# Half products of a DFT as two matmuls of 256 columns instead of one of 512

## The chip, the cores and the metric

One NeuronCore of a Trainium2 chip runs the whole kernel. The metric is the time on the device in microseconds of one execution; lower is better. The core's engines are TensorE (matmuls; the profile calls its matmuls PE and its weight loads PEld), VectorE (DVE), ScalarE (ACT), GpSimd (POOL) and SyncE (SP), which issues the DMAs.

## What is computed

Two branches over one sequence `x` of 2048 rows and 512 columns, mixed by a gate; everything is float32.

```
a = x @ dft_hid_re.T ;  b = x @ dft_hid_im.T
y = dft_seq_re @ a - dft_seq_im @ b                 # real part of a 2-D DFT
q, k, v = heads(x @ wqkv)                           # 32 heads of 16
o = softmax(q k^T / 4) v ;  att = merge(o) @ wo
g = sigmoid((x * gate_w).sum(-1))
out = g * y + (1 - g) * att
```

The change touches the line of `y`, the sequence transform: two products of a 2048 x 2048 matrix with a 2048 x 512 matrix.

## The kernel before

**Precision.** Matmuls of the transforms run in a rounded float32 type. Each factor is split into a high part and the rest, and a product is made of three: high times high, high times rest, rest times high. So one stationary block `h1` (the high part of 128 x 128 of the DFT matrix) is used with the two moving tiles `t[:, 0]` and `t[:, 1]` (high part and rest of 128 rows of `a` or `b`, 512 columns), and `l1` (its rest) with `t[:, 0]`.

**Half products.** TensorE's array has 128 rows. A product over 128 rows is made as two over 64 rows each, in different segments (below), both added into the same PSUM bank. While one half of the array's rows does a half product, the other half does a matmul of the attention, which needs at most 64 rows.

**Stages.** The first 207 us make q, k, v and the imaginary part `b` of the transform over the columns. Then a long middle stage works through the attention's units, two heads at a time, and lays the rest of the transforms beside them. Its work is written out by hand as patterns of slots:

```
FULL = "a5 s4 a2 s0 a3 s6 a5 s4 s1 s0 s2 a6 a3 a4 s5 a1 | |"
```

A pattern is one segment. `a` is a score tile for the row maxima (`a_tile`, matmul at L294, reduced by VectorE at L296), `s` is a score tile for the exponentials (`scores`, matmul at L805, exponentiated by ScalarE at L806), the digit is the PSUM bank, and `|` is the matmuls with the values (`pv`, L851). In each of the 16 slots of FULL one score goes to one half of the rows, and one half product of the sequence transform to the other. The scores come first in the program's order in the first 15 slots and last in the sixteenth. Segments come in pairs: in the second the halves of the rows change places, and the same 16 products get their other half. `take(seq, 16)` gives a pair its 16 products, `segment` sends them out with the scores, and `Chain.mm` (L476) makes the matmul. The first product of a segment waits for a user of the scores of the segment before, so that the two halves of a product don't follow too closely; `segment` puts that dependency on the instruction that `issue` returns.

`dft` yields the products of the sequence transform in their order: for the real part of the DFT matrix (`c = 0`, the first half) and then the imaginary one (`c = 1`, the second half), for each of 16 output tiles `tt`, for each of 16 row tiles `s`, the three products. An output tile is one chain of 48 products in the bank `psD`, 3 pairs of segments long. `dft_next` follows the third product of each `s`: at the end of a chain ScalarE copies the bank out (L531 for `c = 0`, L534 for `c = 1`), and every fourth time GpSimd splits the next chunk of the DFT matrix (L460, L461) and SyncE loads a further one (L450). There are 48 pairs of FULL segments for each half of the transform.

Before the FULL segments come 13 pairs of another pattern with the products of `real` (real part of the transform over the columns), and after them the output projections; both use `Chain.mm` too, with moving tiles 512 columns wide.

The matmuls of the values are float32 as they are, with 17 weights in each of four column groups of the array, and use all 128 rows.

Of the kernel before, what the change touches and what calls it, by code (L numbers as in the profile page):

```python
# [17 lines left out]
D = 512  # L18
# [13 lines left out]
def mix_kernel(ctx: ExitStack, tc: tile.TileContext, xa_t, xa, wqkv, w_hid, w_seq, wo, gate_w, out):  # L32
# [5 lines left out]
    nc = tc.nc  # L38
# [156 lines left out]
    with tc.tile_pool(name="qk", bufs=1, reuse_waits="tile") as pool:  # L195
# [38 lines left out]
        for tb in range(4):  # L234
# [4 lines left out]
            for c in range(2):  # L239
                if tb == 0 and c == 0:  # L240
                    pss = [bank() for _ in range(4)]
                    for kt in range(KT):
                        x = xab[tb][:, :, :, kt * P:(kt + 1) * P]
                        for i, (w, v) in enumerate(((wh, 0), (wl, 0), (wh, 1))):
                            for ct in range(4):
                                nc.tensor.matmul(pss[ct], w[:, c, kt, ct * P:(ct + 1) * P], x[:, :, v],
                                                 start=kt == 0 and i == 0, stop=kt == KT - 1 and i == 2)
# [198 lines left out]
    def c_load(i):  # L446
        if i < len(chunks):
            c, tt, ch = chunks[i]
            raws[i] = work.tile([P, 4, P], F32, name="craw", tag="yr") if i < 2 else spare(i % 2, F32, "craw")
            nc.sync.dma_start(raws[i], w_seq[c, tt, ch])  # L450
# [14 lines left out]
    class Chain:  # L465
# [6 lines left out]
        def mm(self, st, mv, half, stop):  # L472
            if not self.begun:
                self.ps = self.pool.tile([P, 512], F32, name=self.name)
            r = slice(None) if half is None else slice(64 * half, 64 * half + 64)
            i = nc.tensor.matmul(self.ps, st[r], mv[r], start=not self.begun, stop=stop)  # L476
            self.begun = True
            return i

    def real():  # L480

# [8 lines left out]
    def real_next(s, t, chain):  # L490
# [9 lines left out]
        if s == NT - 1:  # L500
# [2 lines left out]
            c_split(2)  # L503
            c_load(4)

    def dft():

        for c in range(2):
            for tt in range(NT):
                chain = Chain(psD, "d", 48)  # L510
                yr = []
                for ch in range(4):
                    i = (c * NT + tt) * 4 + ch
                    h1, l1 = hls.pop(i)
                    if c == 1 and ch == 0:
                        yr.append(work.tile([P, D], F32, name="yr"))
                        nc.sync.dma_start(yr[0], yr_d[tt])
                    for k in range(4):
                        s = 4 * ch + k
                        t = ab[s]  # L520
                        yield chain, h1[:, k], t[:, 0], None
                        yield chain, h1[:, k], t[:, 1], None
                        yield chain, l1[:, k], t[:, 0], partial(dft_next, c, tt, s, t, chain, yr)

    def dft_next(c, tt, s, t, chain, yr):
        if c == 0 and tt == NT - 1:
# [150 lines left out]
    def proj(hf, cts, pools, qts=range(8)):  # L677

        for qt in qts:
            t = hf * 8 + qt  # L680
            chain = Chain(*pools[qt % len(pools)], 3 * len(cts))
            for ct in cts:
                h1, l1 = oh[hf, ct][qt]
                for i, (st, mv) in enumerate(((h1, 0), (h1, 1), (l1, 0))):
                    last = ct == cts[-1] and i == 2
                    yield chain, st, wos[0][:, mv, ct], partial(proj_next, hf, cts, t, chain) if last else None
# [205 lines left out]
    for hf in range(2):  # L892
        for ct in range(4):
            n = 3 if hf and ct == 3 else 4
# [125 lines left out]
    first = proj(0, (0, 1, 2), one * 5 + side[::-1], range(7))  # L1020
    run_plan(0)
    gate()
    hid, seq = real(), dft()


# [59 lines left out]
    for u in range(valued + 2, UNITS, 2):  # L1085
        run_plan(u)
        clock = nc.vector if u == 498 else nc.gpsimd
        i = 0
# [57 lines left out]
```

## Time and profile before

| | |
|---|---|
| two timed runs | 1655.51 and 1655.59 us, median 1655.55 us |
| profiled execution, first to last instruction | 1653.7 us |
| TensorE matmuls, busy | 1646.4 us (100%), 13082 |
| TensorE weight loads, busy | 995.5 us (60%), 13082 |
| VectorE, busy | 1372.1 us (83%) |
| ScalarE, busy | 1264.0 us (76%) |
| GpSimd, busy | 683.8 us (41%) |
| granted clock of TensorE | 0.999 |
| FULL segments of the first half of the transform | 348.92 to 899.90 us, 550.98 us |
| FULL segments of the second half | 899.90 to 1451.30 us, 551.40 us |

The profile is one execution, and its times are counted from its first instruction. A row of a group gives the line of the kernel, the engine, the operation, the tiles written and read, the shape (partitions x elements), the count, and then the busy time in us and the mean length of one in ns. A row of the timeline gives start and length in us first. Lengths of matmuls are modelled and overlap, so what a matmul takes in a row of them is read from one start to the next.

### The profile page before, as it was taken

What the parts mean: (1) busy time and instruction counts of PE and PEld (TensorE: products, weight loads), DVE (VectorE), ACT (ScalarE), POOL (GpSimd) and SP (SyncE); (2) the same over time, 40 slices, a digit from 0 to 9 for tenths busy, and PEclk for the clock granted to TensorE, in tenths of its full rate; (3) what the DMA queues carried; (4) which work ended last, traced back from release to release, by engine and by line L of the source; (5) the groups of instructions that cost most, each with busy time, mean ns of one, the idle gap of its engine ahead of it and who ended that gap; (6) DMA issues with size and microseconds to landing.
All of it is one profiled execution on the core that took longest, in us unless ns stands there. A gap on an engine that the chain in (4) does not pass through costs nothing.

```text
span 1653.7 us, 34501 instructions
## 1 busy us (share of the span) xinstructions
PE 1646.4 (100%) x13082; PEld 995.5 (60%) x13082; DVE 1372.1 (83%) x2338; ACT 1264.0 (76%) x2477; POOL 683.8 (41%) x651
## 2 busy tenths in 40 slices
PE   9999999999999999999999999999999999999998
PEld 7888966655555555555555555555555555544454
DVE  5439888888888888888888888888888888899954
ACT  5312289988888788887888878888788887889996
POOL 0204634443433456434343455544444455333330
PEclk9999999999999999999999999999999999999999
DMA  9977401314141534223147535224141536371014
GB/s 287 355 164 154 160 2 28 51 39 80 58 79 47 98 94 100 71 60 71 41 97 251 106 102 119 66 67 78 51 87 59 113 104 128 130 206 27 23 46 142
DMA packets 85247, 167.17 MB, mean 101 GB/s; under 512 B 22460, under 2 KB 22716, under 8 KB 81068
## 3 DMA queue, kind: packets, MB, share of 16 engines
q1 hardware_dynamic: 84648, 164.30, 39.0%
q8 instruction: 103, 1.69, 0.5%
q10 hardware_dynamic: 432, 0.66, 0.1%
q14 instruction: 64, 0.52, 0.1%
HBM read 109.67 MB, written 55.17 MB: 100 GB/s over the span
## 4 chain that ended last, share of the span: by engine, by line
PE 99%; DMA 0%; DVE 0%; DVEq 0%; ACT 0%; SPq 0%; issue 0%
PE acc L851 28%; PE a L294 23%; PE s L805 21%; PE d L476 9%; PE s L388 3%; PE acc L805 3%; PE acc L294 2%; PE s L422 1%; PE d L388 1%; PE acc L813 1%; PE a L111 1%; PE a L109 1%; PE s L111 1%; PE s L109 1%; PE a L110 1%; PE s L110 1%
## 5 line engine op out<-in xcount | busy, mean ns | idle before, releaser
L296 DVE TENSOR_REDUCE mx<-a 128x1 f32<-128x512 f32 x1828 | 1140.8, 683 | 164.0 <-PE a L294 103.1
L806 ACT ACTIVATE pt<-s 128x512 f32<-128x512 f32 x1792 | 946.4, 628 | 15.2 <-PE s L805 11.2
L294 PE MATMUL a<-ks,qs 64*128 64x512 f32 (+1 forms) x1828 | 677.3, 410 | 0.0
L476 PE MATMUL d<-xab,ch 64*128 64x512 f32 x2016 | 648.5, 396 | 0.0
L805 PE MATMUL s<-qs,ks 64*128 64x512 f32 (+1 forms) x1792 | 583.3, 397 | 0.0
L833 POOL TENSOR_TENSOR oe<-oe,part 128x512 f32<-128x512 f32 x215 | 278.1, 1293 | 653.9 <-ACT part L832 609.3
L851 PE MATMUL acc<-pt,vt 128*17 128x512 f32 x3968 | 479.0, 595 | 0.0
L294 PEld LDWEIGHTS a<-ks,qs 64*128 64x128 f32 (+1 forms) x1828 | 324.1, 184 | 244.6 <-issue 134.4
L476 PE MATMUL d<-xab,cl 64*128 64x512 f32 x1008 | 399.7, 397 | 0.0
L805 PEld LDWEIGHTS s<-qs,ks 64*128 64x128 f32 (+1 forms) x1792 | 321.9, 184 | 84.9 <-ACT pt L806 29.6
L476 PEld LDWEIGHTS d<-xab,ch 64*128 64x128 f32 x2016 | 366.5, 184 | 9.4
L832 ACT COPY part<-acc 128x512 f32<-128x512 f32 x215 | 126.2, 587 | 196.0 <-issue 174.1
L851 PEld LDWEIGHTS acc<-pt,vt 128*17 128x17 f32 x3968 | 89.0, 96 | 228.3 <-issue 148.4
L476 PEld LDWEIGHTS d<-xab,cl 64*128 64x128 f32 x1008 | 185.6, 184 | 5.0
L461 POOL TENSOR_TENSOR cl<-craw,ch 128x512 fp32r<-128x512 f32 x126 | 162.2, 1287 | 10.1
L296 DVE TENSOR_REDUCE mx<-acc 128x1 f32<-128x512 f32 x220 | 151.8, 690 | 12.2
L806 ACT ACTIVATE pt<-acc 128x512 f32<-128x512 f32 x244 | 148.7, 609 | 0.0
L805 PE MATMUL acc<-qs,ks 64*128 64x512 f32 (+1 forms) x244 | 95.5, 391 | 0.0
L294 PE MATMUL acc<-ks,qs 64*128 64x512 f32 (+1 forms) x220 | 85.8, 390 | 0.0
L460 POOL CAST ch<-craw 128x512 fp32r<-128x512 f32 x126 | 77.0, 611 | 18.8 <-PE d L476 13.1
L476 PE MATMUL d<-wre,xab 64*128 64x512 f32 x336 | 81.7, 388 | 0.0
L476 PE MATMUL d<-wo_hl,o_hl 64*128 64x512 f32 x252 | 66.7, 395 | 0.0
(178 smaller groups left out, 1232.5 us busy)
## 6 DMA issues: line engine op xcount, KB each, us to landing
craw<-w_seq SPq DMA_DIRECT2D x128, 256.0 KB
qk<-hl SPq DMA_DIRECT2D x32, 512.0 KB
qs<-qk SPq DMA_DIRECT2D x96, 128.0 KB
ks<-qk SPq DMA_DIRECT2D x96, 128.0 KB
b<-hl SPq DMA_DIRECT2D x16, 512.0 KB
xab<-b SPq DMA_DIRECT2D x16, 512.0 KB
o<-oe SPq DMA_DIRECT2D x62, 128.0 KB
oh<-nh SPq DMA_DIRECT2D x12, 512.0 KB
```

What stands on the lines that cost most here:

```text
L109: nc.tensor.matmul(ps, sh, mh, start=first, stop=False)
L294: nc.tensor.matmul(ps, qs[p % 2][r, qt * P:(qt + 1) * P], ks[p % 2][r, kb * 512:(kb + 1) * 512], start=True, stop=True)
L296: user = nc.vector.tensor_reduce(mx[p % 2][:, h, qt, kb:kb + 1], ps, AX.X, ALU.max)
L388: i = nc.tensor.matmul(ps, st[r], mv[r], start=not half and not j, stop=half == 1 and j == 11)
L460: nc.gpsimd.tensor_copy(h1, raw)
L461: nc.gpsimd.tensor_tensor(l1, raw, h1.bitcast(F32), ALU.subtract)
L476: i = nc.tensor.matmul(self.ps, st[r], mv[r], start=not self.begun, stop=stop)
L805: nc.tensor.matmul(ps, ks[p % 2][rr, kt * P:(kt + 1) * P], qs[p % 2][rr, q0:q0 + 512], start=True, stop=True)
L806: return nc.scalar.activation(pts[u][:, 2 * qb + h], ps, AF.Exp, bias=0.0, scale=DH ** -0.5)
L832: nc.scalar.copy(part[0], acc)
L833: nc.gpsimd.tensor_tensor(total, total, part[0], ALU.add)
L851: i = nc.tensor.matmul(acc[32 * j:32 * j + 17], v[:, 16 * h:16 * h + 17], pt[:, j], start=begin, stop=done or close)
```

## The change

`Chain.mm` accepts a tuple of two moving parts, each with the output columns that it belongs to, and makes one matmul for each, with the same stationary block. The first of the two starts the accumulation, the second ends it, where the one matmul did; the first is the one returned, which carries the dependency. A new function `by_columns` cuts a moving tile into two of 256 columns. In `dft` the third product (`l1` with `t[:, 0]`) is always cut; the first two are cut where `c == 0`. Everything else stays as it is.

```diff
@@ class Chain
             r = slice(None) if half is None else slice(64 * half, 64 * half + 64)
-            i = nc.tensor.matmul(self.ps, st[r], mv[r], start=not self.begun, stop=stop)
+            first = None
+            if isinstance(mv, tuple):
+                for n, (cols, m) in enumerate(mv):
+                    i = nc.tensor.matmul(self.ps[:, cols], st[r], m[r], start=not (self.begun or n),
+                                         stop=stop and n == 1)
+                    first = first or i
+            else:
+                i = first = nc.tensor.matmul(self.ps, st[r], mv[r], start=not self.begun, stop=stop)
             self.begun = True
-            return i
+            return first
...
+    def by_columns(m):
+
+        return tuple((slice(i * D // 2, (i + 1) * D // 2), m[:, i * D // 2:(i + 1) * D // 2]) for i in range(2))
...
@@ def dft
-                        yield chain, h1[:, k], t[:, 0], None
-                        yield chain, h1[:, k], t[:, 1], None
-                        yield chain, l1[:, k], t[:, 0], partial(dft_next, c, tt, s, t, chain, yr)
+                        narrow = by_columns if c == 0 else lambda m: m
+                        yield chain, h1[:, k], narrow(t[:, 0]), None
+                        yield chain, h1[:, k], narrow(t[:, 1]), None
+                        yield chain, l1[:, k], by_columns(t[:, 0]), partial(dft_next, c, tt, s, t, chain, yr)
```

## The prediction

> **What bounds the kernel.** I read the page first, for the engine that the end hangs on, then the busy time of the long middle stage, then that stage matmul by matmul.
>
> ```profile
> span 1653.7 us, 34501 instructions
> PE 1646.4 (100%) x13082; PEld 995.5 (60%) x13082; DVE 1372.1 (83%) x2338; ACT 1264.0 (76%) x2477; POOL 683.8 (41%) x651
> PE 99%; DMA 0%; DVE 0%; DVEq 0%; ACT 0%; SPq 0%; issue 0%
> L476 PE MATMUL d<-xab,ch 64*128 64x512 f32 x2016 | 648.5, 396 | 0.0
> L476 PE MATMUL d<-xab,cl 64*128 64x512 f32 x1008 | 399.7, 397 | 0.0
> L476 PEld LDWEIGHTS d<-xab,ch 64*128 64x128 f32 x2016 | 366.5, 184 | 9.4
> ```
>
> The chain that ends last is TensorE for 99% of the span, so a change of matmuls counts at full weight unless the array does something else meanwhile. There are as many weight loads as matmuls (13082 each): one load goes with every matmul. The half products of the sequence transform are the two L476 matmul groups, 64 rows high and 512 columns wide, 2016 + 1008, and 48 more of the first two chunks stand under another tile name: 3072 half products, two for each of 1536 products. They fill the 96 pairs of segments of the full pattern, which last from 348.92 to 1451.30 us; the first half of the transform (c = 0) is the first 96 segments.
>
> ```profile
> 348.92:899.90 550.98, 550.98 (x4612) 318.87 (x4608) 485.89 (x830) 449.46 (x880) 242.37 (x228) 1.00 0.35 82
> 899.90:1451.30 551.40, 551.40 (x4614) 318.82 (x4610) 486.90 (x833) 449.55 (x880) 266.32 (x247) 1.00 0.40 99
> ```
>
> The columns after the length are the busy times of PE, PEld, DVE, ACT and POOL, then the granted clock. A segment takes 550.98 / 96 = 5.739 us and the clock is 1.00 throughout. DVE works 485.89 / 96 = 5.06 us of a segment, ACT 4.68, so TensorE sets the pace and the others have 0.68 us or more to spare. One segment, TensorE matmuls alone (start, length):
>
> ```profile
> 601.46 0.49 PE L294 MATMUL a<-ks,qs 64*128 64x512 f32 x1
> 601.47 0.49 PE L476 MATMUL d<-xab,ch 64*128 64x512 f32 x1
> 601.79 0.39 PE L805 MATMUL s<-qs,ks 64*128 64x512 f32 x1
> 601.80 0.39 PE L476 MATMUL d<-xab,cl 64*128 64x512 f32 x1
> 602.02 0.39 PE L294 MATMUL a<-ks,qs 64*128 64x512 f32 x1
> 602.03 0.39 PE L476 MATMUL d<-xab,ch 64*128 64x512 f32 x1
> 602.26 0.39 PE L805 MATMUL s<-qs,ks 64*128 64x512 f32 x1
> 602.27 0.39 PE L476 MATMUL d<-xab,ch 64*128 64x512 f32 x1
> ...
> 604.11 0.39 PE L476 MATMUL d<-xab,ch 64*128 64x512 f32 x1
> 604.11 0.39 PE L294 MATMUL acc<-ks,qs 64*128 64x512 f32 x1
> 604.33 0.39 PE L476 MATMUL d<-xab,ch 64*128 64x512 f32 x1
> ...
> 605.03 0.39 PE L476 MATMUL d<-xab,ch 64*128 64x512 f32 x1
> 605.04 0.39 PE L294 MATMUL a<-ks,qs 64*128 64x512 f32 x1
> 605.35 1.91 PE L851 MATMUL acc<-pt,vt 128*17 128x512 f32 x16
> 607.20 0.50 PE L294 MATMUL a<-ks,qs 64*128 64x512 f32 x1
> ```
>
> A product (L476) and a score (L294 or L805) start within 0.01 us of each other on the two halves of the rows and run side by side; I call that a slot. The recorded lengths (0.39) overlap, so only starts count. Products start at 601.80 and, as the fifteenth of the segment, at 605.03: 14 steps in 3.23 us, 0.231 us a slot. Over the stage it is the same: 5.739 less the values block (605.35 to 607.20, 1.85), the first slot (0.33) and the last with its drain (0.32) leaves 3.24 us for 14 steps, 0.2314 us. Single steps run from 0.22 (604.11 to 604.33) to 0.24 (602.03 to 602.27).
>
> **The change, part by part.** It moves no DMA, no wait and no operation of another engine. It makes 768 products × 2 halves = 1536 half products of the first half, and every third of the second half's 1536, 512, into two matmuls of 256 columns with the same weights: 2048 more matmuls and 2048 more weight loads. The score beside each stays 512 wide. The dependency of a segment's first product stays on the first of the two; its second follows on the same queue and waits for nothing new. The matmul that ends a chain is still its last, so the copies of L531 and L534 start where they did.
>
> The columns are the same in number. What can cost is the second load and the second start.
>
> *The load.* It can lie under the matmul before it, as the loads of a segment's start show:
>
> ```profile
> 601.46 0.18 PEld L476 LDWEIGHTS d<-xab,ch 64*128 64x128 f32 x1
> 601.57 0.19 PEld L476 LDWEIGHTS d<-xab,cl 64*128 64x128 f32 x1
> 601.80 0.18 PEld L476 LDWEIGHTS d<-xab,ch 64*128 64x128 f32 x1
> 1644.05 0.97 PEld L739 LDWEIGHTS s<-pairsum,oe 128*128 128x128 f32 x8 [0.25 <-ACT oe L733]
> 1644.08 1.08 PE L739 MATMUL s<-pairsum,oe 128*128 128x64 f32 x8
> ```
>
> The load for the next product (601.57) starts 0.11 us after the one before, while the product of the same half that began at 601.47 is still on the array, and the one after that starts at 601.80 together with its predecessor's matmul: a half takes its next weights behind its own running matmul. How short can a load with its matmul be? L739 has matmuls of only 64 columns, each with a load of 128 weights: eight loads begin in 0.97 − 0.19 = 0.78 us, 7 steps of 0.111 us. Two loads thus need 0.22 us: less than the slot of 0.2314. The second load stays hidden; if that cover were gone it would cost the whole 0.11 us, 2048 × 0.11 = 225 us.
>
> *The start.* No matmul of 256 columns is in this trace, so I bound it by its neighbours in width. With no second stream beside it a matmul of 512 columns with its load takes:
>
> ```profile
> 92.95 14.21 PE L422 MATMUL s<-wv,xab 128*128 128x512 f32 x62
> ```
>
> (14.21 − 0.39) / 61 = 0.2266 us. So of a slot's 231.4 ns, 4.8 ns come from the company of the other half. There are stretches without them:
>
> ```profile
> 402.08 0.39 PE L476 MATMUL d<-xab,ch 64*128 64x512 f32 x1
> 402.98 0.39 PE L476 MATMUL d<-xab,cl 64*128 64x512 f32 x1
> ```
>
> The second row is the fourth product after the first: 0.90 / 4 = 0.225 us a slot, with both halves busy. For what a further start adds, the low end is nothing. The high end is the spread of one and the same instruction, 0.225 to 0.24 us, 15 ns: that much can a step lose by the way its start falls. I take the middle, 7 ns (an estimate). Alone, a narrow pair then takes 226.6 + 7 = 233.6 ns, 2 ns more than the 231.4 at which the score beside it goes anyway; so 4.8 of the 7 lie beside the score, as long as the company of the score does not cost the narrow pair its 4.8 ns as well. 2048 × 2 ns = 4.1 us; without that cover it would be 14 us.
>
> *A narrow matmul in the middle of a wide one.* The second of the pair starts when the score is half done. That the halves can run so is shown in an earlier stage, where a product and a score start 0.12 us apart and neither loses its pace (L476 217.18 to 217.41, L805 217.06 to 217.30):
>
> ```profile
> 217.06 0.39 PE L805 MATMUL s<-qs,ks 50*128 50x512 f32 x1
> 217.18 0.39 PE L476 MATMUL d<-wre,xab 64*128 64x512 f32 x1
> 217.30 0.39 PE L805 MATMUL acc<-qs,ks 50*128 50x512 f32 x1
> 217.41 0.39 PE L476 MATMUL d<-wre,xab 64*128 64x512 f32 x1
> ```
>
> *First and last slot, values.* The first slot is long because its load lies open (601.46 to 601.57); the second narrow matmul there finds its load hidden under the first. The last slot ends with the wide score (605.04) before the values. Nothing there changes.
>
> *The sum.* Against the profiled execution, 1653.7 + 4.1 = 1657.8 us of span. The two timed runs (1655.51 and 1655.59 us, median 1655.55) stand 1.85 us above that span, so the forecast is 1659.6, rounded to **1659 us**. Its own range, 0 to 6 ns a slot, is 1655 to 1668.
>
> **The rivals.**
>
> *Faster: the halves get out of each other's way.* The 4.8 ns of company may come from two 512-column streams that run in step. If narrow products bring all narrowed slots to 226.6 ns, 2048 × 4.8 = 9.8 us are won: 1646 us. It decides where the narrow pair itself fits into 226.6 ns, that is where a further start costs nothing. For it: the score's 512 columns alone would allow it. Against: the two streams that stand half a matmul apart at 217.06 keep 0.23 to 0.24, so falling out of step is not enough. With the 225 of the good stretch it would be 1642.
>
> *Slower: every start is paid.* If the steps of 0.24 are what an ill-placed start costs, and each of the two narrow matmuls is as exposed as the one wide one was, a slot grows by 6 ns (its mean above the 225 of the good stretch) to 15: 12 to 31 us, 1668 to 1686, 1677 in the middle. It decides from the point at which the pair exceeds the 231.4 of the score. For it: the products and the scores slow down together in the rows above. Against: the single stream at L422 has no such spread, so the start as such is not the cause.
>
> *Much slower: a straight line, or the issue.* If the time of a matmul with its load lay on the line from 111 ns at 64 columns to 226.6 at 512, one of 256 would take 161 ns, a pair 322, 91 ns over the slot: 186 us, 1842 us. And if TensorE's issue set the pace (a segment has 96 loads and matmuls, 59.8 ns each), 128 of them would take 7.65 us in the first half, and the whole change would cost 4096 × 59.8 ns = 245 us: 1900 us. Against the line: the row of 64 columns is the loads' own pace. Against the issue: L422's stage needs only two instructions per 226.6 ns and a slot four in 231.4, so it isn't their number that sets the step.
>
> A fixed part in each matmul is also what the Trainium skill states, in TensorEngine Tiling (Array Packing), section Instruction Overhead, against this change: each matmul has some 60 cycles of overhead. At the 2.4 GHz that TensorE: Matmul & The Clock Gate gives, that is an estimated 25 ns a start, 51 us, 1707 us. By the same clock 512 columns are 213 ns, and L422's 226.6 leave 13 ns over them; the trace does not bear the rule out for matmuls that follow one another, and 256 columns are in any case not in it.
>
> *That the change doesn't do what it says* would be equal weights loaded once for both narrow matmuls: L422 has neighbours with equal weights too, and loads and matmuls are still 13082 each, so I give it nothing of its own; it would only make the forecast surer.
>
> **How the numbers follow.** The forecast (1655 to 1668) has 0.47, the faster rival 0.23, every start paid 0.23, the last two together 0.07, for what can bend the line part of the way as well. The range must leave out no more than 2 in 10: it takes in the faster rival from 1643 and the slower up to its end, with a little beyond, and leaves out the long shots and the edges of both, about 0.12. About 2% (33 us) is what a measurement of this kernel can tell from no change: slower than 1688.7 is 0.07 and a little of the third case, 0.08; faster than 1622.4 has no mechanism with a price, 0.01; within it 0.91.
>
> **What would show it.** In the changed profile TensorE should have 2048 more matmuls and loads (15130 each), the narrow ones as 64x256. In a segment of the first half the second narrow product should start about 0.115 us after the first, in the middle of the score, and the score's step should be 0.231 to 0.235 us; the segments of the second half should lie between that and 5.744 us. The step at 0.227 would prove the faster rival, 0.24 to 0.246 the slower. If the load of the second narrow product starts only when the first has ended, the cover has failed, and the step is 0.34. DVE's and ACT's busy time should not move. I am wrong if 256 columns cost far more than half of 512, which no row here measures, or if the score waits for the product beside it.

## The result and the profile after

| | before | after |
|---|---|---|
| two timed runs, median | 1655.55 us | 1670.22 us (1670.13 and 1670.32) |
| ratio after / before | | 1.0091, 95% interval 1.0072 to 1.0110 |
| profiled execution, first to last instruction | 1653.7 us | 1668.5 us |

The kernel became 14.7 us slower, 0.9%: clearly more than nothing, and less than the 2% bound. That is 7.2 ns for each of the 2048 further matmuls. The forecast was 1659 us; the time lies 11 us above it, inside the range given (from 1643 to a little beyond 1686), but outside the forecast's own 1655 to 1668. It is the slower rival's territory (1668 to 1686).

The page of the changed kernel: span, busy times, the chain that ended last, and the groups of half products.

```profile
span 1668.5 us, 38597 instructions
PE 1660.5 (100%) x15130; PEld 1123.8 (67%) x15130; DVE 1373.0 (82%) x2338; ACT 1264.3 (76%) x2477; POOL 683.8 (41%) x651
PE 99%; DMA 0%; DVE 0%; DVEq 0%; issue 0%
L479 PE MATMUL d<-xab,cl 64*128 64x256 f32 x2016 | 405.5, 281 | 0.0
L483 PE MATMUL d<-xab,ch 64*128 64x512 f32 x1024 | 331.6, 398 | 0.0
L479 PE MATMUL d<-xab,ch 64*128 64x256 f32 x1984 | 327.8, 283 | 0.0
```

TensorE has 15130 matmuls and 15130 loads, 2048 more of each. DVE, ACT and POOL have the instructions and busy times they had. TensorE is still 99% of the chain, so its own steps must account for the whole loss. The two halves of the transform, as windows over the changed kernel (length, then busy time of PE, PEld, DVE, ACT, POOL, then the granted clock):

```profile
349.30:912.68 563.38, 563.38 (x6148) 409.24 (x6145) 486.27 (x830) 449.45 (x880) 242.81 (x228) 1.00 0.34 81
912.68:1466.15 553.47, 553.47 (x5124) 356.68 (x5120) 487.15 (x832) 449.54 (x880) 265.86 (x247) 1.00 0.40 98
```

Before, both windows together were 550.98 + 551.40 = 1102.38 us, 5.741 us a segment in each half. Now a segment takes 563.38 / 96 = 5.869 us in the first half (+0.127) and 553.47 / 96 = 5.765 in the second (+0.024). The sum is 1116.85, so 14.5 of the 14.8 us of span lie in these 192 segments, 12.2 of them in the first half. The clock is 1.00 as before. One segment of the first half, TensorE's matmuls (start, length; "x2" is the two narrow ones of a product in one row):

```profile
601.59 0.50 PE L294 MATMUL a<-ks,qs 64*128 64x512 f32 x1
601.59 0.50 PE L479 MATMUL d<-xab,ch 64*128 64x256 f32 x2
601.92 0.39 PE L817 MATMUL s<-qs,ks 64*128 64x512 f32 x1
601.93 0.40 PE L479 MATMUL d<-xab,ch 64*128 64x256 f32 x2
602.15 0.39 PE L294 MATMUL a<-ks,qs 64*128 64x512 f32 x1
602.17 0.40 PE L479 MATMUL d<-xab,cl 64*128 64x256 f32 x2
...
605.17 0.38 PE L294 MATMUL a<-ks,qs 64*128 64x512 f32 x1
605.29 0.40 PE L479 MATMUL d<-xab,ch 64*128 64x256 f32 x2
605.61 0.62 PE L863 MATMUL acc<-pt,vt 128*17 128x512 f32 x4
```

Read the two columns of starts apart. The scores go from 601.92 to 605.17 in 14 steps: 0.232 us, the pace they had. The products go from 601.93 to 605.29 in 14 steps: 0.240 us. They begin the second slot together and are 0.12 us apart in the sixteenth. Before, score and product ended side by side; now the products' half of the array ends last, and the values (605.61) wait for it. The single narrow steps are 120 ns with hardly any spread (the middle 90% of 2784 steps in the first half are all 120). So the loss is 14 × (0.240 − 0.2314) = 0.12 us a segment, on the products' side alone.

In the second half every third product is narrow:

```profile
1104.01 0.40 PE L479 MATMUL d<-xab,cl 64*128 64x256 f32 x2
1104.24 0.39 PE L483 MATMUL d<-xab,ch 64*128 64x512 f32 x1
1104.48 0.39 PE L483 MATMUL d<-xab,ch 64*128 64x512 f32 x1
1104.71 0.39 PE L479 MATMUL d<-xab,cl 64*128 64x256 f32 x2
```

Three slots take 0.70 us, 0.233 each, and the narrow one is no longer than the wide ones. So all three are longer than the 0.231 of before: over all segments of this half the narrow pair takes 232.7 ns, the wide product after it 233.5 and the one before the next pair 232.7. The loss of a segment there, 0.024 us over 16 / 3 narrow slots, is 4.5 ns for each of them, and most of it lies in the wide products; in the first half it is 0.127 / 16 = 7.9 ns.

### The profile page after: what moved, and what is told of

It reads as the page before. It is cut to its first block, busy times and chain, and to the rows that moved or that the text cites. A ratio compares the mean times of both kernels' runs of the same rounds, so it can differ in the third digit from the quotient of the medians.

```text
span 1668.5 us, 38597 instructions
## 1 busy us (share of the span) xinstructions
PE 1660.5 (100%) x15130; PEld 1123.8 (67%) x15130; DVE 1373.0 (82%) x2338; ACT 1264.3 (76%) x2477; POOL 683.8 (41%) x651
## 4 chain that ended last, share of the span: by engine, by line
PE 99%; DMA 0%; DVE 0%; DVEq 0%; issue 0%
PE acc L863 28%; PE a L294 19%; PE s L817 16%; PE d L479 15%; PE d L483 6%; PE s L388 3%; PE acc L817 2%; PE acc L294 2%; PE s L422 1%; PE d L388 1%; PE acc L825 1%; PE a L110 1%; PE a L109 1%; PE s L110 1%; PE s L109 1%; PE a L111 1%
## 5 line engine op out<-in xcount | busy, mean ns | idle before, releaser
L479 PE MATMUL d<-xab,cl 64*128 64x256 f32 x2016 | 405.5, 281 | 0.0
L479 PEld LDWEIGHTS d<-xab,cl 64*128 64x128 f32 x2016 | 338.6, 186 | 5.7
L483 PE MATMUL d<-xab,ch 64*128 64x512 f32 x1024 | 331.6, 398 | 0.0
L479 PE MATMUL d<-xab,ch 64*128 64x256 f32 x1984 | 327.8, 283 | 0.0
L479 PEld LDWEIGHTS d<-xab,ch 64*128 64x128 f32 x1984 | 272.7, 188 | 0.0
L461 POOL TENSOR_TENSOR cl<-craw,ch 128x512 fp32r<-128x512 f32 x126 | 162.2, 1287 | 10.1
L483 PEld LDWEIGHTS d<-xab,ch 64*128 64x128 f32 x1024 | 156.7, 185 | 0.0
```

The source lines that it names most:

```text
L461: nc.gpsimd.tensor_tensor(l1, raw, h1.bitcast(F32), ALU.subtract)
L479: i = nc.tensor.matmul(self.ps[:, cols], st[r], m[r], start=not (self.begun or n), stop=stop and n == 1)
L483: i = first = nc.tensor.matmul(self.ps, st[r], mv[r], start=not self.begun, stop=stop)
```

## The experiments

Ten kernels in four groups: where the loss sits, what a matmul costs by its columns, what its weights do, and which half of the array owns the price. Where a kernel has one run, it is read by its segments, which agree between kernels to about 0.01 us where nothing is changed (5.736 to 5.744 us for wide second halves). The unchanged work ahead of the full segments ends at 349 us in some kernels and at 351 in others, so one total can be 2 us off for that alone.

### One half of the transform at a time

**All products narrow in the first half, all wide in the second.**

```diff
-                        yield chain, l1[:, k], by_columns(t[:, 0]), partial(...)
+                        yield chain, l1[:, k], narrow(t[:, 0]), partial(...)
```

> The products of the first half of the sequence transform stay cut in two, those of the second half are all one matmul again (1536 further matmuls instead of 2048). In the changed kernel a segment of the first half took 5.869 us against 5.741 before, 96 of them. Start theory (every product matmul pays some 13 ns besides its columns, so two of 256 take 2 x 120 = 240 ns where the slot had 231, and the products' half sets the pace): the first half keeps its 96 x 0.127 = 12.2 us, the second gives back its 2.3 us: 1667.8 us. Equal price for each further matmul (14.67 us / 2048 = 7.2 ns): 1655.55 + 11.0 = 1666.6 us. Second-half segments back at 5.741 us by both.

Measured: 1669.42 us (four runs, 1667.71 to 1670.03), ratio 1.0082 (1.0068 to 1.0096).

```profile
351.00:914.37 563.37, 563.37 (x6148) 409.27 (x6144) 486.26 (x830) 449.45 (x880) 242.60 (x228) 1.00 0.35 80
914.37:1465.19 550.82, 550.82 (x4612) 321.06 (x4608) 487.08 (x832) 449.55 (x880) 265.82 (x247) 1.00 0.40 99
```

Its segments take 5.868 us in the first half and 5.738 in the second: the first half's loss is that of the full change, and the second half's is gone. The 1.6 us over the expected total lies ahead of the segments, which begin at 351.0 us here and at 349.3 in the changed kernel.

**Every third product narrow in both halves.**

```diff
-                        narrow = by_columns if c == 0 else lambda m: m
+                        narrow = lambda m: m
```

> Only every third product is cut, in both halves (1024 further matmuls). Start theory with a catch-up (between two cut products the two wide ones can run at the 226.6 ns of a lone stream, so the mean of three stays near the score's 231): as the changed kernel's second half, 24 ns a segment: 192 x 24 ns = 4.6 us, 1660.1 us. Equal price of 7.2 ns each: 7.3 us, 1662.9 us. A price of 7.9 ns each, as in the first half of the changed kernel: 8.1 us, 1663.7 us.

Measured: 1660.93 us (six runs), ratio 1.0034 (1.0022 to 1.0046).

```profile
348.71:902.47 553.76, 553.76 (x5126) 356.77 (x5122) 486.26 (x830) 449.58 (x880) 242.68 (x228) 1.00 0.35 82
902.47:1455.95 553.48, 553.48 (x5125) 356.32 (x5121) 487.18 (x832) 449.59 (x880) 265.95 (x247) 1.00 0.40 98
```

Both halves take 5.77 us a segment (the mean is 5.767), as the second half of the change does. An equal price of 7.2 ns for each narrow slot would make 5.780; the segments speak against it, and so does the median (1662.9 us were expected then), though the interval of the total reaches to 1663.2. Spread thin, a narrow product costs about 5 ns, and here too the wide products beside it step at 233 ns and not at 231. Why they do is open.

**Two of three narrow in the first half, all narrow in the second.**

```diff
-                        narrow = by_columns if c == 0 else lambda m: m
-                        yield chain, h1[:, k], narrow(t[:, 0]), None
+                        narrow = by_columns if c == 1 else lambda m: m
+                        yield chain, h1[:, k], by_columns(t[:, 0]), None
```

> First half: two of three products cut (first and third), second half: all of them (2560 further matmuls). Start theory with catch-up: 240, 240 and 226.6 ns make 235.5 a slot against 231.4, 66 ns a segment, 6.3 us for the first half; the second half all cut, as the first half of the changed kernel, 12.2 us: 1674.1 us, first-half segments 5.807 us, second-half segments 5.869 us. Price in proportion to the number cut (7.9 ns each): first-half segments 5.826 us, 1675.9 us. If it mattered which of the two halves of the transform is cut, second-half segments would differ from 5.869 us.

Measured: 1676.39 us (four runs), ratio 1.0126 (1.0112 to 1.0140).

```profile
349.63:908.88 559.25, 559.25 (x5636) 389.71 (x5633) 486.27 (x830) 449.68 (x880) 242.67 (x228) 1.00 0.35 81
908.88:1472.31 563.43, 563.43 (x6150) 409.18 (x6146) 487.17 (x832) 449.49 (x880) 266.07 (x247) 1.00 0.39 97
```

All narrow in the second half gives 5.869 us, the first half's figure: it is the number of narrow products that matters, not the half. Two thirds give 5.826, two thirds of the full loss (7.9 ns for each narrow slot). So the wide product between two narrow ones catches nothing up (it takes 233 ns, the two pairs 241 and 237); only with two wide ones after it is the narrow one cheaper.

### What a narrow matmul costs by its columns

In these kernels the first product of each chain keeps all its columns, as two matmuls of 256, so that every column of the bank is begun; but for it, the second half is wide.

**Two of 192 columns** (columns 192 to 255 and 448 to 511 of the other products left out).

```diff
+        return tuple((slice(a, b), m[:, a:b]) for a, b in ((0, 192), (256, 448)))
```

> First half only: the two matmuls of a product take 192 columns each (columns 192 to 255 and 448 to 511 of a product are left out, but for each chain's first product, which is whole), second half wide. It tells a pace of the loads from a price of the start. Load theory (120 ns is how fast loads of 128 weights follow one another on one half while the other half loads too): the step stays at 120 ns, segments at 5.87 us, 1667.8 us. Start theory (13 ns and 0.416 ns a column, by 120 ns at 256 and 226.6 at 512): 93 ns of array time, held back by the loads at the 111 ns that 64 columns took: step 111 to 113 ns, the pair under the score's 231, segments at 5.74 us, 1655.6 us.

Measured: 1655.00 us; segments of 550.75 / 96 = 5.737 us in the first half. The products' matmuls and their loads:

```profile
602.17 0.39 PE L479 MATMUL d<-xab,ch 64*128 64x192 f32 x2
602.40 0.27 PE L479 MATMUL d<-xab,ch 64*128 64x192 f32 x1
602.51 0.27 PE L479 MATMUL d<-xab,cl 64*128 64x192 f32 x1
602.62 0.27 PE L479 MATMUL d<-xab,cl 64*128 64x192 f32 x1
```

```profile
602.20 0.30 PEld L479 LDWEIGHTS d<-xab,ch 64*128 64x128 f32 x2
602.42 0.30 PEld L479 LDWEIGHTS d<-xab,cl 64*128 64x128 f32 x2
602.64 0.30 PEld L479 LDWEIGHTS d<-xab,ch 64*128 64x128 f32 x2
```

The mean step is 111.5 ns, and two loads take 0.22 us: the loads stand end to end, at the pace that the prediction read off L739. This settles that doubling the loads and the starts is free as long as the products' half stays within the scores' 231 ns: 2 × 111.5 = 223 does. And it shows that the loads' pace is 111.5, not 120, so at 256 columns the loads do not set the step.

**Two of 320 columns**, overlapping in the middle.

```diff
+        return tuple((slice(a, b), m[:, a:b]) for a, b in ((0, 320), (192, 512)))
```

> First half only: the two matmuls of a product take 320 columns each and overlap by 128 (columns 192 to 319 are added twice, but for each chain's first product, which is two of 256), second half wide. With 320 columns a load has time to finish. Start theory (13.4 ns + 0.4164 ns a column, the line through 120 at 256 and 226.6 at 512): 146.7 ns a step, 293 a pair, 62 over the slot: 96 x 16 x 62 ns = 95 us, 1751 us. No fixed part (226.6 x 320 / 512): 141.6 ns, 283 a pair, 79 us, 1735 us; then the 120 at 256 columns would be the loads' pace.

Measured: 1748.57 us, segments of 6.712 us.

```profile
600.82 0.31 PE L479 MATMUL d<-xab,ch 64*128 64x320 f32 x1
600.96 0.31 PE L479 MATMUL d<-xab,cl 64*128 64x320 f32 x1
601.11 0.31 PE L479 MATMUL d<-xab,cl 64*128 64x320 f32 x1
601.26 0.31 PE L479 MATMUL d<-xab,ch 64*128 64x320 f32 x1
```

The mean of 2784 steps is 146.5 ns. With 119.9 at 256 columns, 64 columns are 26.6 ns, 0.416 ns each, and a part of 13.4 ns is left that does not go with the columns. Carried on to 512 columns this line gives 226.3 ns; L422's matmuls, 128 rows high, took 226.6. So one line, 13.4 + 0.416 × columns, holds at 256 and 320 columns on 64 rows and at 512 on 128 rows. At 512 on 64 rows, 231 ns, it does not (see the 480 columns below). A step proportional to the columns (226.6 × 320 / 512 = 141.6 ns) falls.

The Trainium skill's TensorE: Matmul & The Clock Gate, section Back-to-back issue gap, gives columns / 2.4 + 2.5 ns for an isolated matmul: an estimated 109 ns for 256 and 136 for 320. The trace agrees with the slope and not with the constant, 13.4 where each matmul has a load of its own. The 25 ns a start that the prediction estimated from the Trainium skill's TensorEngine Tiling (Array Packing), section Instruction Overhead, are about twice the 13.4.

**One of 480 columns** (columns 480 to 511 left out).

```diff
+        return tuple((slice(a, b), m[:, a:b]) for a, b in ((0, 480),))
```

> The half products of the first half as one matmul of 480 columns (columns 480 to 511 left out but in the first product of each chain), the second half wide. The time is that of before in every theory, about 1655 us, since the scores stay at 231 ns a slot; what tells is the step of the products where they do not wait. By the law from 256 columns, 480 x 0.4164 + 13.3 = 213 ns, and the products get ahead of the scores within a segment. If a wide matmul on 64 rows has 4 to 5 ns of its own besides, 217 to 218 ns.

Measured: 1654.71 us, segments of 550.38 / 96 = 5.733 us.

```profile
601.60 0.38 PE L479 MATMUL d<-xab,cl 64*128 64x480 f32 x1
601.80 2.48 DVE L296 TENSOR_REDUCE mx<-a 128x1 f32<-128x512 f32 x4 [0.69 <-PE a L294]
...
604.21 0.42 PE L479 MATMUL d<-xab,cl 64*128 64x480 f32 x1
...
604.35 0.18 PEld L479 LDWEIGHTS d<-xab,ch 64*128 64x128 f32 x1
...
604.48 0.38 PE L479 MATMUL d<-xab,ch 64*128 64x480 f32 x1
```

From the product at 601.60 to that at 604.21 are 12 steps in 2.61 us: 217.5 ns, where the line gives 213. A wide matmul on 64 rows has 4 to 5 ns of its own over the line, at 480 columns as at 512 (231 against 226.6). The step to the product at 604.48 is a stall, 0.27 us. The products are 0.18 us ahead of the scores by then, but the lead does not seem to be what stops them: in the middle 90% of the stalls it lies anywhere from 0.13 to 0.18 us. What stays the same is the time since a reduction of VectorE. This is the product of the fifteenth slot, whose score (`s5`), before it in the program, writes the bank that the fourth reduction of the segment (`a5`) reads. That reduction ends at 601.80 + 2.48 = 604.28; the product's load begins 0.07 us later, and the product 0.20. In 93 of the 96 segments there is a stall at this place, and in the middle 90% of them the product starts 0.186 to 0.201 us after the end of that reduction. So the trace points to the score's wait for its bank, behind which the product stands; no run tests it. Products faster than the scores gain nothing.

### What the weights do

**96 of the 128 weights, and 72 of them**, both with two matmuls of 256 columns in the first half and a wide second half (the other 32 or 56 output rows get only the first product of a chain and its last). The second differs by its number alone.

```diff
+            rows = slice(0, 96 if self.begun and not stop else P)
...
+                    i = nc.tensor.matmul(self.ps[rows, cols], st[r, rows], m[r], start=not (self.begun or n),
```

> First half only: the products are cut into two of 256 columns, and the matmuls have 96 weights a row instead of 128 (96 of the 128 output rows; the other 32 are left out, but for the first product of a chain and its last matmuls), second half wide. A load of 96 weights is a quarter shorter. Start theory: the step stays at 120 ns, 1667.8 us. Load theory: the load no longer holds the pair up, the step falls to the columns' time, 107 to 113 ns, the pair under the score's 231 ns, segments at 5.74 us, 1655.6 us.

> All half products of the first half as two matmuls of 256 columns, the second half wide; each product but the first and the last of a chain loads and uses 72 of its 128 weights (the other 56 output rows get no further products). The price goes with the weights: 106.7 ns of columns + 13.3 x 72 / 128 = 7.5 ns gives a step of 114 ns, a pair of 228, less than the score's 231: segments of the first half at 5.74 us, the whole about 1655 us. A part of the price is fixed per start (the line through 13.2 ns at 128 weights and 9.7 ns at 96 with its slope halved below them): step 117 to 119 ns, pair 234 to 238, segments of 5.78 to 5.84 us, 1660 to 1666 us.

Measured: 1657.75 and 1658.81 us. The first-half windows of the two, in that order:

```profile
350.98:902.93 551.95, 551.95 (x6149) 395.37 (x6146) 485.69 (x830) 449.42 (x880) 242.44 (x228) 1.00 0.35 82
```

```profile
351.34:903.26 551.92, 551.92 (x6149) 393.43 (x6145) 486.12 (x830) 449.43 (x880) 242.41 (x228) 1.00 0.36 82
```

Both give 5.749 us a segment instead of 5.869: nearly all of the loss is gone (of the totals, another 2 us are the segments' later start, at 351 us). The mean step is 116.4 ns with 96 weights and 116.9 with 72. After the first of them the price looked proportional to the weights (13.4 × 96 / 128 = 10.1 ns over the columns, 9.9 measured); the second refutes that, since it should have come to 114. About 10 ns belong to a narrow matmul at 72 and at 96 weights alike. Some 3 ns more appear with all 128 weights when narrow matmuls follow without a break; with every third product narrow, 128 weights too, the steps are 115.6 and 117.2. Those 3 ns decide the first half, since 2 × 116.5 = 233 almost fits beside the score and 240 does not. Their mechanism is not settled: with the weights the output rows become fewer too, so the two runs do not even tell whether the load or the output matters.

### Which half of the array owns the price

**Scores alone**: 14 of 16 products in each segment of the first half left out, all others wide.

```diff
+                chain.alone = c == 0
...
+                if x and getattr(x[0], "alone", False) and 0 < n < 15:
+                    if stop and x[3]:
+                        x[3]()
+                    x = None
```

> All products are one matmul as before the change; in the first half the 14 middle products of every segment are left out, so that 14 of 16 scores run with nothing on the other half of the rows. Company theory of the prediction (4.8 of a slot's 231.4 ns come from the stream on the other half): the scores step at 226.6 ns, first-half segments 14 x 4.8 = 67 ns shorter, 5.674 us, 1649.1 us. If the company costs nothing and the scores' own stream goes at 231: 5.741 us, 1655.6 us. Less than 226.6 would mean that the lone stream of the early stage is held back by something else.

Measured: 1654.86 us, the same as the run of the kernel before beside it.

```profile
348.90:899.90 551.00, 551.00 (x3270) 314.52 (x3268) 485.73 (x830) 449.60 (x882) 242.18 (x228) 1.00 0.35 82
```

The trace has 1342 matmuls fewer than before in this window, and not 0.1 us is won. The scores alone go at 231.1 ns. The "company" of the other half, from which the prediction took its 4.8 ns of cover and its faster rival, is not there.

**Products alone**: 14 of 16 scores of each full segment only 64 columns wide (their other columns are left out; the exponentials and the maxima read the 64 eight times over). Products all narrow in the first half, all wide in the second.

```diff
+        w = 64 if short_score else 512
-        nc.tensor.matmul(ps, ks[p % 2][rr, kt * P:(kt + 1) * P], qs[p % 2][rr, q0:q0 + 512], start=True, stop=True)
+        nc.tensor.matmul(ps[:, :w], ks[p % 2][rr, kt * P:(kt + 1) * P], qs[p % 2][rr, q0:q0 + w], start=True, stop=True)
```

> All half products of the first half narrow, the second half wide, and 14 of the 16 scores of each full segment 64 columns wide instead of 512 (their other columns are left out; the exponentials and the maxima read the 64 columns eight times over, so ScalarE and VectorE keep their work). The products have the array to themselves but for a load and 64 columns in each slot. If the price is the products' own: narrow steps of 120 ns, wide ones of 231, segments of 5.87 and 5.74 us, 1669 us, as with all of the first half narrow. If it comes from the scores beside them: wide steps at 226.6, as in the stage of L422, and narrow ones at 113 to 116, segments of 5.67 and 5.68 to 5.75 us, 1646 us or somewhat less.

Measured: 1666.52 us.

```profile
349.20:912.58 563.38, 563.38 (x6148) 409.24 (x6144) 481.75 (x830) 442.64 (x880) 242.71 (x228) 1.00 0.35 80
912.58:1462.39 549.81, 549.81 (x4612) 347.86 (x4608) 477.96 (x832) 442.61 (x880) 265.76 (x247) 1.00 0.41 99
```

```profile
603.47 0.28 PE L482 MATMUL d<-xab,ch 64*128 64x256 f32 x1
603.59 0.28 PE L482 MATMUL d<-xab,cl 64*128 64x256 f32 x1
603.71 0.28 PE L482 MATMUL d<-xab,cl 64*128 64x256 f32 x1
603.83 0.28 PE L482 MATMUL d<-xab,ch 64*128 64x256 f32 x1
```

The first-half window is that of the changed kernel to the last digit, 563.38 us, with no more than a load and 64 columns of a score beside most products. Narrow steps are 119.9 ns, wide ones 230.7 (5.727 us a segment). The scores' loads, which this kernel keeps, are not the cause either: of its 2784 narrow steps 388 have no load of a score beginning in them or in the 0.12 us before, and these take 120.0 ns. So the price is the products' own, and in the first half a slot is as long as the dearer of its two halves.

The way of the change can therefore not beat the kernel before: whatever is done to the products, the scores hold their half for 231 ns a slot.

## Why the prediction was right or wrong

- **TensorE is the bound, 2048 matmuls and loads come on top, nothing else moves:** right, by the page's counts and busy times.
- **The second load is hidden:** right. With 192 columns two loads end to end cost nothing, and with 256 the step is 120 ns, not the 0.34 us a slot of a failed cover.
- **A narrow matmul may start in the middle of the score:** right. The score's step stayed 0.231 to 0.232.
- **First and last slot unchanged:** wrong by little. The last slot now ends with the products, and the values start 0.32 us after the last pair's first start, as before, but that start is 0.12 us later.
- **The start, 7 ns of 0 to 15:** the term that was mis-sized. A narrow pair takes 240 ns in the first half; against 226.6 that is 13.4 for the second start, nearly the upper end. The spread of steps, from which the bound was taken, has nothing to do with it: it is there when the scores run alone (0.226 to 0.236 for the middle 90%). The 13 ns stood in L422's row all along, as what 226.6 leaves over the columns; the prediction named them, but only against the 25 ns, and put them neither into the bounds nor into the sum.
- **The cover of 4.8 ns:** the number holds for another reason. A wide matmul on 64 rows takes 231 ns by itself, not 226.6 and company. Counted from the 230.7 of a wide product beside short scores, the second start costs 240 − 230.7 = 9 ns, not far from the 7 of the prediction, and the cover is 0.7 and not 4.8; then the cover is the term that failed. Which count is the right one depends on why a wide matmul on 64 rows takes longer than the line, and that is open. By both, the score gives the products 231.4 ns, and 240 − 231.4 = 8.6 is paid in the 14 steps, where the prediction had 2. With the right start the sum would have been 1536 × 14 / 16 × 8.6 ns = 11.6 us for the first half; measured 12.2. The prediction also counts 16 slots of a segment where 14 steps pay, and writes 1659.6 as 1659; both are small.
- **One price for every narrow slot:** wrong in the second half. There a narrow product costs 4.5 to 5 ns: its pair takes 233 and not 240, and the two wide products beside it take 233 and not 231, which the prediction has nowhere. Put at 8.6 too, the second half would have lost 3.9 us; it lost 2.3.
- **The rivals:** "every start is paid" gave the size (6 ns a slot and more, 1668 and up), and 0.240 was named as its sign; but its reason, the chance of an ill-placed start, falls: the narrow steps are all 120. That the time lies in the range given is thus in part luck: the range reached that far for a reason that does not hold. The rival's condition, a pair beyond the score's 231.4, was the right one. "The halves get out of each other's way" falls with the company. The straight line through 64 columns falls, since that row is the loads' pace; the issue's pace falls with the free doubling at 192 columns.

## What to carry to other kernels

A matmul that loads its own weights has a part that no column count takes away; read it off two widths of one stream, or off one row as the time left over its columns (0.416 ns each here), and put it into the sum for every further matmul. Where two halves of the rows run side by side, work out the pace of each half by itself and take the slower: slack on one half is the only thing that pays for more instructions there. Here the scores hold a slot at 231 ns and a wide product takes as much, so there is next to no slack: a pair of 192 columns (223 ns) is free, and a pair of 240 ns is paid in full beyond 231.

## What the runs showed of the hardware that was not expected

- A stream of matmuls with 128 weights each goes at 13.4 + 0.416 ns per column (on 64 rows 119.9 at 256 columns and 146.5 at 320, on 128 rows 226.6 at 512), down to a loads' pace of 111.5 ns.
- Wide matmuls on 64 rows are 4 to 5 ns slower than that line: 231 at 512 and 217.5 at 480 columns, with or without work on the other half. Why is open.
- The fixed part of a narrow matmul falls to about 10 ns with 96 weights or with 72, and with 128 weights where only every third product is narrow. What the other 3 ns wait for is open; the loads' pace alone is not it, since 320 columns, which leave a load 35 ns of room, pay 13.4 as well.
- With every third product narrow, the wide ones between take 233 ns too, where they take 231 among themselves. Why is open.
- The products of 480 columns stall in nearly every segment at the same place, and go on 0.19 us after VectorE's last read of the bank that the score before them writes; their lead over the scores varies there from 0.13 to 0.18 us.
